# Three x tiles of the first attention batches transposed by DMA where TensorE and VectorE did it

## The chip, the cores and the metric

The kernel runs on one core of a Trainium2 chip. The metric is the device time of one execution in microseconds; before the change it is 313.5 us, the median of three runs (312.98 to 313.79). The profiled execution spans 311.5 us, and all positions in time below are counted from the start of that span.

## The reference

Causal attention with a decaying bias feeds a two-layer feed-forward network with exact GELU. The attention has 8 batches, 8 heads, 576 positions and 64 values per head; the network has 4608 tokens, a width of 512 and an inner width of 2048.

```python
scores = scale * q @ k.T + minimum(-(cum[i] - cum[j]), 0)   # cum = cumsum(max(s, 0))
attn   = softmax(where(j > i, -1e9, scores))
x      = (attn @ v).transpose(0, 2, 1, 3).reshape(4608, 512)
h      = x @ w_in
out    = (0.5 * h * (1 + erf(h / sqrt(2)))) @ w_out
```

Matmuls are done in bf16 with fp32 accumulation.

## The kernel before

The tokens are numbered batch after batch. Attention works on a batch b in query tiles `it` of 128 rows (tiles 0 to 3) and one of 64 rows (tile 4). The network works on nine chunks c of 512 tokens. Since a batch has 576 tokens, chunk 1 takes its columns 512 to 1023 from batch 0's tile 4 (columns 512 to 575), and from batch 1's tiles 0 to 3 (from column 576 on).

The program is one long stream, written out by hand under a manual schedule: each engine does its instructions in the order of the program, and semaphores join the engines. The loop `for c in range(NCH)` does layer 1 of chunk c, then layer 2 of chunk c with the attention of batch c + 1 placed between its matmuls. The lists `side[0]` to `side[15]` say what comes after each sixteenth of layer 2. For chunk 0, `groups(c, (0, 1), side[:8])` does layer 2's row blocks ("subs") 0 and 1 together with the first eight lists, and then sub 2 and sub 3 take four lists each.

The pieces that matter here:

- `sc_item` (sc): scores of four heads by TensorE (line 349), exponential by ScalarE (line 364). `mk_item` (mk): the causal mask, by VectorE (lines 372 and 377). `scale_v`: v times a weight, by VectorE (line 224).
- `av_item` (av): attention rows of one tile and four heads g, by TensorE (line 440); VectorE divides (lines 449 and 450) and writes x, of which there are six buffers. When the second group of heads (g = 1) of a tile is done, `to_xT` follows at once, unless the caller passes `later=True`.
- `to_xT` puts x, whose rows are tokens, into xT, whose rows are the 512 values of x: `xT[:, ko, token]`. With `pe=True` TensorE does four transposes into a PSUM tile (line 415) and VectorE copies it to xT (line 418). The PSUM tile shares two buffers with the attention rows (tag "av"). Without it SyncE issues one DMA transpose from x to xT (line 411).
- `l1_item`: layer 1, TensorE (line 472) and GELU by ScalarE (line 477). It reads all 512 columns of a chunk at once. `l2_item`: layer 2, TensorE (line 488). At the end of a sub ScalarE (chunk 0, line 498) or VectorE (line 500) copies to o_sb, of which there are three buffers, and SyncE stores it (line 502).
- GpSimd issues the loads of q, k and v and of the weights (lines 106, 122, 148). SyncE's queue holds the output stores and the DMA transposes, in the order of the program.

All tiles of batch 0, and tiles 0 to 3 of batch 1, are transposed by TensorE before the change. From tile 4 of batch 1 on, all go by DMA: 31 DMA transposes, of which the first is issued at 60.9 us.

Of the kernel before, what the change touches and what calls it, by code (L numbers as in the profile page):

```python
# [19 lines left out]
def kernel(  # L20
# [89 lines left out]
    def load_qks(b):  # L110
        load_qk(b, 0)
        load_qk(b, 1)
# [5 lines left out]
    def load_v(b, eng, sts=range(ST)):  # L118
        t = raws[b, "v"] if (b, "v") in raws else raw_v(b)
        for st in sts:  # L120
            n_st = 128 if st < ST - 1 else SL
            eng.dma_start(  # L122
                out=t[:n_st, st, :, :],
                in_=bass.AP(
                    tensor=v.tensor,
                    offset=v.offset + b * H * S * D + st * 128 * D,
                    ap=[[D, n_st], [S * D, H], [1, D]],
                ),
            )
# [56 lines left out]
    def tr_qk(b, i, g):  # L186

        nc.vector.transpose(  # L188
            qkT[b % 2][:, i, g, :S, :].rearrange("p s e -> p (s e)").bitcast(fp32)
            .rearrange("p (l j) -> p j l", j=LT),  # L190
            raws[b, "qk"][:, i, g, :].bitcast(fp32).rearrange("p (j w) -> p j w", j=LT),
        )
# [20 lines left out]
    def square_v(b, st):  # L213
        n_st = 128 if st < ST - 1 else SL
        sq = work.tile([128, H * D], bf16, tag="sq", bufs=2, name="sq")
        nc.scalar.activation(  # L216
            sq[:n_st], raws[b, "v"][:n_st, st].rearrange("p h d -> p (h d)"), func=AF.Square,
            accum_out=sumv[:n_st, b, st : st + 1],
        )

    def scale_v(b, st, eng=nc.vector):
        n_st = 128 if st < ST - 1 else SL
        w = wb[:n_st, st, b * H : (b + 1) * H]
        eng.tensor_tensor(  # L224
            vv[b % 2][:n_st, st, :, 0:D],
            raws[b, "v"][:n_st, st, :, :],
            w.unsqueeze(2).to_broadcast([n_st, H, D]),
            op=MULT,
        )

    def den_col(b):
        nc.vector.tensor_copy(vv[b % 2][:, :, :, D], wb[:, :, b * H : (b + 1) * H])
# [228 lines left out]
    def l1_item(c, f2, n0=0, n1=NB):  # L461
        if f2 == 0 and n0 == 0:
            gT_of[c] = work.tile([128, FT, NB], bf16, tag="gT", bufs=1, name="gT")
        if n1 - n0 < NB and f2 % 4 < 2:
            h_ps = yps.tile([128, 2, NB // 2], fp32, tag="mlp", bufs=2, name="h2_ps")
        else:
            h_ps = ps.tile([128, 2, NB], fp32, tag="sc", bufs=2, name="h_ps")
        h_ps = h_ps[:, :, : n1 - n0]
        for i in range(2):
            ft = f2 * 2 + i  # L470
            for ko in range(KO):
                nc.tensor.matmul(  # L472
                    h_ps[:, i, :], lhsT=w_in_r[:, ko, ft * 128 : (ft + 1) * 128],
                    rhs=xT[:, ko, c * NB + n0 : c * NB + n1],
                    start=(ko == 0), stop=(ko == KO - 1),
                )
        nc.scalar.activation(  # L477
            gT_of[c][:, f2 * 2 : f2 * 2 + 2, n0:n1], h_ps, func=AF.Gelu
        )
# [24 lines left out]
    def exp_set():  # L504
        nc.scalar.preload_act_table_set("natural_log_exp_and_others")  # L505
# [67 lines left out]
    sc, mk, av = sc_item, mk_item, av_item  # L573
# [5 lines left out]
    for c in range(NCH):  # L579
        b = c + 1  # L580
        if c > 0 and b + 1 < B:
            load_qks(b + 1)
            load_v(b + 1, nc.gpsimd)
        if c == 0:

            late = [
                [], [], [], [], [(av, 0, 0, 2), (av, 0, 1, 2)],
                [(av, 0, 0, 3), (av, 0, 1, 3)], [(to_xT, 0, 2, True), (to_xT, 0, 3, True)],
                [], [(scale_v, 0, 4), (av, 0, 0, 4)], [(av, 0, 1, 4)],
            ] + [[]] * 6  # L590
            for half in range(2):
                for f2 in range(FT // 2):
                    l1_item(0, f2, half * 256, half * 256 + 256)
                    for f, *a in late[8 * half + f2]:
                        f(*a)
                    if f2 % 2 and 3 <= 8 * half + f2 <= 11:
                        square_v(0, 4 * half + f2 // 2 - 1)
        else:
            for f2 in range(FT // 2):
                l1_item(c, f2)  # L600
                for g, it in late_of.get(c, [])[f2 : f2 + 1]:
                    av(c, g, it)
                if b < B and f2 < HG:
                    tr_qk(b, 0, f2)
                    tr_qk(b, 1, f2)
                if b < B and f2 == 2:
                    den_col(b)
                    for st in range(2):
                        scale_v(b, st)
                if b < B and f2 == 3:  # L610
                    for st in range(2, ST):
                        scale_v(b, st)
                if b < B and 4 <= f2 < 4 + HG:
                    absmax(b, f2 - 4)
                if c == 2 and f2 == 7:
                    cert_decay()
                if f2 < ST and c < B:
                    square_v(c, f2)
        if b < B:
            if c == 0:  # L620
                for g in range(HG):
                    for i in range(2):
                        tr_qk(b, i, g)
                den_col(b)
            exp_set()
            if c == 0:
                load_qks(2)
                load_v(2, nc.gpsimd)
                side = [[] for _ in range(16)]
                side[0] = [(sc, b, 0, 0), (mk, b, 0, 0)]  # L630
                side[3] = [
                    (sc, b, 1, 0), (to_xT, 0, 4, True), (scale_v, b, 0), (scale_v, b, 1), (mk, b, 1, 0)
                ]
                side[5] = [(sc, b, 0, 1), (av, b, 0, 0), (av, b, 0, 1)]
                side[6] = [(av, b, 1, 0, True), (av, b, 1, 1, True), (scale_v, b, 2), (mk, b, 0, 1)]
                side[7] = [(to_xT, b, 0, True), (sc, b, 1, 1)]
                side[8] = [(to_xT, b, 1, True), (scale_v, b, 3), (av, b, 0, 2), (gelu_set,), (mk, b, 1, 1)]
                side[9] = [(av, b, 0, 3)]
                side[11] = [(av, b, 1, 2, True), (scale_v, b, 4), (square_qk, 0, 0, 0), (square_qk, 0, 0, 1)]
                side[12] = [(av, b, 1, 3, True), (square_qk, 0, 1, 0), (square_qk, 0, 1, 1)]  # L640
                side[13] = [(to_xT, b, 2, True)]
                side[14] = [(to_xT, b, 3, True)]
                groups(c, (0, 1), side[:8])
                for sub in (2, 3):
                    groups(c, (sub,), side[4 * sub : 4 * sub + 4])
            else:

                side = [[] for _ in range(16)]
                sc_at = (1, 4, 6, 8) if b < 4 else (1, 4, 7, 10)
                for at, (g, u) in zip(sc_at, [(0, 0), (1, 0), (0, 1), (1, 1)]):  # L650
                    side[at].append((sc, b, g, u))
                side[sc_at[3]].append((gelu_set,))
                mk_at = (4, 6, 8, 10) if b < 4 else (4, 7, 10, 13)
                for at, (g, u) in zip(mk_at, [(0, 0), (1, 0), (0, 1), (1, 1)]):
                    side[at].append((mk, b, g, u))
                for at, (g, it) in zip((5, 6, 8, 9), [(0, 0), (0, 1), (1, 0), (1, 1)]):
                    side[at].append((av, b, g, it))
                if b < 4:
                    side[10].append((av, b, 0, 2))
                    side[11].append((av, b, 1, 2))  # L660

                    side[15].extend([(av, b, 0, 3), (av, b, 1, 3)])
                if c == 1:
                    side[0].append((absmax, c, 0))
                    side[12].extend([(square_qk, c, 1, 0), (square_qk, c, 1, 1)])
                    side[3].append((cert_exp,))
                for sub in range(4):
                    groups(c, (sub,), side[4 * sub : 4 * sub + 4])
        else:
            for sub in range(4):  # L670
                l2_item(c, (sub,), store=(c, sub) < LAST)
                if c == B - 1:
                    (cert_1, cert_2, cert_3, cert_4)[sub]()
                elif sub == 0:

                    rv = nc.values_load(bad[0:1, 0:1], min_val=0, max_val=1)
# [169 lines left out]
```

## Time and profile before

| what | value |
|---|---|
| time | 313.5 us (312.98 to 313.79) |
| span of the profiled execution | 311.5 us |
| TensorE transposes (line 415) | 36, for nine tiles |
| VectorE copies to xT (line 418) | 9: 424 ns for 128 rows, 292 ns for 64 |
| DMA transposes (line 411) | 31, median 2.4 us from issue to landing, longest 7.0 |
| layer 2 of chunk 0 | from 35.6 us |
| layer 1 of chunk 1 | from 55.34 us |

The page gives each engine's busy time as a share of the span. A matmul's record lasts from its start until its result is there, and the next starts before that, so TensorE's cost of a piece is read from its start to the start of the next piece. A row by time has the start, the length of the group, the engine, the line and the operation, and in brackets an idle time ahead of it with what ended it. In the DMA view q0 is the queue of the transfers that GpSimd issues and q1 that of SyncE's; "share" is the time their packets took, over 16 DMA engines, and since packets overlap it can be over 100%. Packets as small as four bytes are the semaphores' and not data.

### The profile page before, as it was taken

To read this page: it belongs to the slowest core of one execution; us is meant where nothing else is said; L and a number is where in the kernel's file an instruction comes from. 1 tells how busy PE (TensorE), PEld (TensorE's weight loads), DVE (VectorE), ACT (ScalarE), POOL (GpSimd) and SP (SyncE) were. 2 spreads that over 40 slices of the span, in tenths; PEclk is the share of its full clock that TensorE was granted. 3 is DMA by queue.
4 is the path that set the end of the run, shared out by engine and by line. 5 is a ranking of instruction groups with operands and counts; after the bars stand their busy time and mean duration, and the time that the engine had idled before them with its cause. 6 is when DMAs were issued, how large, how long until landed. Compare 5 with 4: busy or idle time off the path is not lost. (4 is left out here: it accounts for less than half of the span.)

```text
span 311.5 us, 6102 instructions
## 1 busy us (share of the span) xinstructions
PE 303.9 (98%) x2511; PEld 155.1 (50%) x2511; DVE 195.2 (63%) x397; ACT 193.3 (62%) x262; POOL 53.1 (17%) x72
## 2 busy tenths in 40 slices
PE   6999999999999999999999999999999999999994
PEld 2479755444554455445454545444544555444441
DVE  6786577697769775966498549955895632250010
ACT  1787878878848772974687548765776657105500
POOL 7473250142002400060007000500000000000000
PEclk9999999999999999999999999999999999999999
DMA  8999999769641974089208941623101311010012
GB/s 144 214 231 206 225 219 283 160 140 197 165 98 17 211 173 118 8 180 208 87 18 175 220 93 31 146 66 103 51 19 42 103 53 25 34 68 36 0 69 76
DMA packets 33027, 36.73 MB, mean 118 GB/s; under 512 B 17760, under 2 KB 22112, under 8 KB 32992
## 3 DMA queue, kind: packets, MB, share of 16 engines
q0 software_dynamic: 11472, 22.81, 37.5%
q1 hardware_dynamic: 20336, 12.93, 14.7%
q10 hardware_dynamic: 1184, 0.52, 0.6%
q8 instruction: 21, 0.34, 0.4%
q14 instruction: 14, 0.11, 0.1%
HBM read 36.85 MB, written 9.44 MB: 149 GB/s over the span
## 5 line engine op out<-in xcount | busy, mean ns | idle before, releaser
L488 PE MATMUL o_ps<-w_out_r,gT 128*128 128x512 bf16 x576 | 135.6, 379 | 0.0
L472 PE MATMUL h_ps<-xT,w_in_r 128*128 128x512 bf16 (+1 forms) x640 | 131.6, 358 | 0.0
L477 ACT ACTIVATE gT<-h_ps 128x1024 bf16<-128x1024 f32 (+1 forms) x80 | 75.1, 938 | 65.7 <-PE h_ps L472 64.7
L472 PEld LDWEIGHTS <-w_in_r 128*128 128x128 bf16 x640 | 60.0, 98 | 54.3 <-issue 0.3
L488 PEld LDWEIGHTS <-gT 128*128 128x128 bf16 x576 | 52.0, 98 | 56.9 <-issue 2.8
L364 ACT ACTIVATE P<-sc_ps 128x1024 bf16<-128x1024 f32 x56 | 54.3, 1021 | 25.3 <-PE sc_ps L349 25.2
L500 DVE COPY o_sb<-o_ps 128x512 f32<-128x512 f32 x30 | 20.7, 692 | 55.7 <-PE o_ps L488 55.7
L122 POOL DMA_DIRECT2D raw_v<-in_v_dram x39 | 33.1, 859 | 125.8 <-ACT sq L216 115.2
L188 DVE STREAM_TRANSPOSE qkT<-raw_qk 128x576 f32<-128x576 f32 x32 | 37.0, 1237 | 0.0
L449 DVE RECIPROCAL rc<-av 128x4 f32<-128x4 f32 (+1 forms) x80 | 14.1, 176 | 35.1 <-PE av L440 35.0
L450 DVE TENSOR_TENSOR x<-av,rc 128x256 bf16<-128x256 f32 (+1 forms) x80 | 33.8, 423 | 3.0
L440 PEld LDWEIGHTS <-P 128*128 128x128 bf16 x576 | 26.5, 98 | 15.8 <-DVE P L372 1.4
L208 DVE TENSOR_REDUCE amx<-raw_qk 128x2 f32<-128x2304 bf16 x13 | 32.6, 2534 | 0.0
L440 PE MATMUL av<-vv,P 128*128 128x65 bf16 x576 | 30.2, 193 | 0.1
L372 DVE TENSOR_TENSOR P<-P,tri_bf 128x1024 bf16<-128x1024 bf16 (+1 forms) x33 | 22.0, 670 | 6.6 <-ACT P L364 5.9
L224 DVE TENSOR_TENSOR vv<-raw_v,wb 128x512 bf16<-128x512 f32 (+1 forms) x39 | 25.2, 691 | 0.4 <-DMA raw_v<-in_v_dram 0.4
L216 ACT ACTIVATE sq<-raw_v 128x512 bf16<-128x512 f32 (+1 forms) x40 | 24.8, 621 | 0.0
L349 PE MATMUL sc_ps<-qkT 32*128 32x256 bf16 (+2 forms) x560 | 18.1, 250 | 0.0
L349 PEld LDWEIGHTS <-qkT 32*128 32x128 bf16 x560 | 11.8, 92 | 12.2 <-issue 8.9
L505 ACT ACT_TABLE_LOAD x8 | 10.3, 1283 | 1.3 <-PEq L830 1.2
L424 PE MATMUL f_ps<-zero 128*128 128x512 bf16 x30 | 9.7, 449 | 1.2 <-DVE zero L151 1.2
L508 ACT ACT_TABLE_LOAD x8 | 10.3, 1283 | 0.1
(80 smaller groups left out, 92.1 us busy)
## 6 DMA issues: line engine op xcount, KB each, us to landing
out_dram<-o_sb SPq DMA_DIRECT2D x34, 256.0 KB, 2.2
raw_v<-in_v_dram POOLq DMA_DIRECT2D x31, 256.0 KB, 5.6
raw_qk<-in_q_dram POOLq DMA_DIRECT2D x7, 576.0 KB, 7.5
raw_qk<-in_k_dram POOLq DMA_DIRECT2D x7, 576.0 KB, 10.7
w_in_r<-in_moe_w_in_dram POOLq DMA_DIRECT2D x4, 512.0 KB, 10.6
w_out_r<-in_moe_w_out_dram POOLq DMA_DIRECT2D x4, 512.0 KB, 16.8
raw_v<-in_v_dram POOLq DMA_DIRECT2D x8, 128.0 KB, 6.1
raw_qk<-in_q_dram POOLq DMA_DIRECT2D x2, 288.0 KB, 6.1
```

Of the source, the lines that this page charges most:

```text
L122: eng.dma_start(out=t[:n_st, st, :, :], in_=bass.AP(tensor=v.tensor, offset=v.offset + b * H * S * D + st * 128 * D, ap=[[D, n_st], [S * D ...
L188: nc.vector.transpose(qkT[b % 2][:, i, g, :S, :].rearrange("p s e -> p (s e)").bitcast(fp32) .rearrange("p (l j) -> p j l", j=LT), raws[b, ...
L208: nc.vector.tensor_reduce(amx[:, b * HG + g], raws[b, "qk"][:, :, g, :], axis=AX, op=ALU.max, apply_absolute_value=True,)
L216: nc.scalar.activation(sq[:n_st], raws[b, "v"][:n_st, st].rearrange("p h d -> p (h d)"), func=AF.Square, accum_out=sumv[:n_st, b, st : st ...
L224: eng.tensor_tensor(vv[b % 2][:n_st, st, :, 0:D], raws[b, "v"][:n_st, st, :, :], w.unsqueeze(2).to_broadcast([n_st, H, D]), op=MULT,)
L349: nc.tensor.matmul(s_ps[h // 2][:, h % 2, off : off + n], lhsT=qk[r, 1, g, jt * 128 : jt * 128 + 128, e], rhs=qk[r, 0, g, i0 : i0 + n, e], ...
L364: nc.scalar.activation(P[:, 2 * h2 : 2 * h2 + 2, o : o + 512], s_ps[h2], func=AF.Exp, scale=scale)
L440: nc.tensor.matmul(o_ps[:, h, :], lhsT=P[:, h, off : off + 128], rhs=vv[b % 2][:, jt, 4 * g + h, :], start=(i == 0), stop=(i == len(BLK[it ...
L450: nc.vector.tensor_tensor(x_of[b, it][:n, g * 256 : g * 256 + 256].rearrange("p (h d) -> p h d", d=D), o_ps[:n, :, 0:D], rc[:n].unsqueeze( ...
L472: nc.tensor.matmul(h_ps[:, i, :], lhsT=w_in_r[:, ko, ft * 128 : (ft + 1) * 128], rhs=xT[:, ko, c * NB + n0 : c * NB + n1], start=(ko == 0) ...
L477: nc.scalar.activation(gT_of[c][:, f2 * 2 : f2 * 2 + 2, n0:n1], h_ps, func=AF.Gelu)
L488: nc.tensor.matmul(y_of[c, sub], lhsT=gT[:, ft, sub * 128 : (sub + 1) * 128], rhs=w_out_r[:, ft, :], start=(ft == 0), stop=(ft == FT - 1),)
```

## The change

Three tiles that chunk 1 needs, tile 4 of batch 0 and tiles 0 and 1 of batch 1, are transposed by DMA in place of TensorE and VectorE. This is to take twelve transposes off TensorE and three copies off VectorE. The tiles of batch 1 are issued directly when their attention rows are done (`later` is no longer passed), tile 4 of batch 0 is moved from `side[3]` to `side[7]`. Tiles 2 and 3 of batch 1 stay as they were.

```diff
                 side[3] = [
-                    (sc, b, 1, 0), (to_xT, 0, 4, True), (scale_v, b, 0), (scale_v, b, 1), (mk, b, 1, 0)
+                    (sc, b, 1, 0), (scale_v, b, 0), (scale_v, b, 1), (mk, b, 1, 0),
                 ]
                 side[5] = [(sc, b, 0, 1), (av, b, 0, 0), (av, b, 0, 1)]
-                side[6] = [(av, b, 1, 0, True), (av, b, 1, 1, True), (scale_v, b, 2), (mk, b, 0, 1)]
-                side[7] = [(to_xT, b, 0, True), (sc, b, 1, 1)]
-                side[8] = [(to_xT, b, 1, True), (scale_v, b, 3), (av, b, 0, 2), (gelu_set,), (mk, b, 1, 1)]
+                side[6] = [(av, b, 1, 0), (av, b, 1, 1), (scale_v, b, 2), (mk, b, 0, 1)]
+                side[7] = [(to_xT, 0, 4), (sc, b, 1, 1)]
+                side[8] = [(scale_v, b, 3), (av, b, 0, 2), (gelu_set,), (mk, b, 1, 1)]
```

## The prediction

> **What bounds the kernel now.** I read the busy shares first, then the list of waits, then the stretch from 36 to 56 us, where layer 2 of chunk 0 runs: TensorE by time, SyncE by time, and the DMA queues by window.
>
> ```profile
> PE 303.9 (98%) x2511; PEld 155.1 (50%) x2511; DVE 195.2 (63%) x397; ACT 193.3 (62%) x262; POOL 53.1 (17%) x72
> ```
>
> TensorE is busy from end to end. Its queue is in order, so time taken out of it anywhere, or put in, moves the end by as much, unless a later idle place absorbs it. The list of waits has none of size on TensorE: its longest entries are other engines that wait for TensorE (ACT gT 64.7 us, DVE o_sb 55.7 us). Eight matmuls of chunk 1's layer 1 start at 57.31 us and the attention row behind them at 59.04: 1.73 us, 216 ns each, the full rate. So I find nothing later that gives time back.
>
> TensorE by time, in the stretch that is changed (start, length, engine, line, operation):
>
> ```profile
> 40.41 0.29 PE L415 MATMUL xt_ps<-ident_bf,x 64*128 64x64 bf16 x4
> 40.63 1.90 PE L488 MATMUL o_ps<-w_out_r,gT 128*128 128x512 bf16 x8
> ...
> 45.76 0.39 PE L415 MATMUL xt_ps<-ident_bf,x 128*128 128x128 bf16 x4
> 46.08 0.64 PE L349 MATMUL sc_ps<-qkT 32*128 32x256 bf16 x24
> ...
> 47.52 0.39 PE L415 MATMUL xt_ps<-ident_bf,x 128*128 128x128 bf16 x4
> 47.75 0.41 PE L440 MATMUL av<-vv,P 128*128 128x65 bf16 x8
> ...
> 54.48 1.03 PE L488 MATMUL o_ps<-w_out_r,gT 128*128 128x512 bf16 x4
> 55.34 1.03 PE L472 MATMUL h_ps<-xT,w_in_r 128*128 128x512 bf16 x4
> ```
>
> What counts is from start to next start, since the matmuls overlap: a tile's four transposes hold the queue for 0.22, 0.32 and 0.23 us. At 55.34 us chunk 1 begins; its first matmul reads xT columns 512 to 1023, to which all three changed tiles belong.
>
> The DMA engines in the same stretch, in two windows (queue: packets, MB, share):
>
> ```profile
> q0 software_dynamic: 293, 0.66, 110.8%
> ...
> out_dram<-o_sb SPq DMA_DIRECT2D x2, 256.0 KB, 8.2
> ```
>
> ```profile
> q0 software_dynamic: 350, 1.05, 67.6%
> q1 hardware_dynamic: 335, 0.62, 33.9%
> ...
> out_dram<-o_sb SPq DMA_DIRECT2D x1, 256.0 KB, 6.6
> ```
>
> The first is 46 to 49 us, the second 49.5 to 55 us. q0 carries GpSimd's loads (q, k and v of batch 2, issued from 36.6 to 46.4 us, landing 12 to 13.5 us later); q1 carries what SyncE issues. Two output stores were issued at 46.37 us, yet until 49 us q1 has no packet at all: nearly 3 us in which the loads ahead are served. From then on q1 gets about one packet for each of q0. So these stores land 7.3 and 8.2 us after issue (53.7 and 55.0 us), where the whole kernel's median is 2.2. The DMA share is above 1.0 until 54 us, 0.63 in 55 to 56 and 0.40 in 56 to 57.
>
> **What the Trainium skill says.** "VectorE: DVE Perf Modes", section The three transpose paths, prices one 128x128 bf16 transpose at 390 ns on TensorE and 1309 ns by DMA. The trace has the same order of size: 0.39 us for four overlapping on TensorE, 1.19 us of SyncE's queue for one DMA transpose of a whole tile. "DMA: Bandwidth & Descriptors", section Queues, rings and completion order, says that a DMA engine alternates between the queues that have work, packet by packet; the 335 against 350 packets above agree. "TensorE: Matmul & The Clock Gate", Part 1, says that TensorE's clock halves after an idle window of some 3.4 us and comes back after about as long busy. The opening agrees in part: the warming matmuls (line 424) run at 4 per us from 2 to 5 us, then 7 in the next, and after the idle from 6.30 to 8.45 us the rate is still full.
>
> **The change part by part.**
>
> *Removed from TensorE:* twelve transposes of three tiles, 0.22 + 0.32 + 0.23 = 0.77 us of queue. The attention matmuls that follow at 48.85 us take 0.38 us for eight, where the like ones take 0.24; they wait for scale_v of tile 3 (ending at 48.97 us), which sits behind the two removed copies on VectorE (0.42 us each). With these gone that 0.14 us goes too. Sum 0.9 us. The attention matmuls at 44.30 us still wait 0.24 us for x, as before.
>
> *Removed from VectorE:* copies of 0.29 + 0.42 + 0.42 = 1.13 us. VectorE idles here for other engines (3.9 us before the mask at 39.70), so beyond the 0.14 they are worth nothing.
>
> *Moved:* three tiles go to SyncE's queue. The order of instructions of the changed kernel there is: transpose (1,0), transpose (1,1), store of sub 0, store of sub 1, transpose (0,4), store of sub 2. Its waits show the first weight load of chunk 1 waiting for exactly the three transposes. Behind that weight load, on TensorE's in-order queue, stands all of layer 1 of chunk 1, hence GELU on ScalarE, and the late attention rows that VectorE reads.
>
> *When TensorE asks:* 55.34 - 0.9 = 54.4 us.
>
> *When the tiles are there:* x of (1,0) is written at 45.27 us, of (1,1) at 45.82, both some 0.2 earlier now. Issues: 45.1 and 46.3 us (1.2 us each, from the two at 81.60 us that take 2.50), stores from 47.5, transpose (0,4) at about 48.4. It is the oldest tile but the last in the queue, behind both stores. The nearest row is the one DMA transpose under load, of 64 rows too, with nothing ahead of it on SyncE's queue:
>
> ```profile
> xT<-x SPq DMA_TRANSPOSE x1, 7.0
> ```
>
> It was issued at 60.89 us. Unloaded ones land after 2.4. That would put (1,0) at 52.1 us or later, and (0,4), were it alone, at 48.4 + 7.0 = 55.4.
>
> Lower bound for (0,4): before, the second store landed at 55.0 us. Its queue now starts 1.3 us earlier (45.1 for 46.37) but has two whole transposes ahead, which at the unloaded pace of 1.25 us each are 2.5: 56.2. Then the half transpose, about 0.6 at that pace: 56.8 us. Upper bound: the 256-byte packets of the transposes (about 512 for a whole tile, by the 1104 packets under 512 B around the pair at 81.6, so 32 on each of 16 engines) alternate one for one with the loads' packets, of which about 28 per engine are left at 48 us (98 in the us before 49, 350 in 49.5 to 55, over 16), so the first transpose is done only when the loads are, at 55.5; then the second (1.0), two stores (1.0 each), the half one (0.6) and the way to the semaphore, 0.8: 60 us. If several small packets pass for each large one it is nearer the lower. I take 58.2, a little under the middle, 58.4.
>
> *Net:* chunk 1 starts at 58.2 and not 55.34: +2.9 us; TensorE idles 58.2 - 54.4 = 3.8 us. For the clock I take nothing, as the windows of the skill's page are fixed in time and an idle of 3.8 us rarely holds a whole one; the other end is the opening's loss, 3.5 us at half rate, 1.75 us.
>
> **The rivals.**
>
> *A, forecast: the wait is longer than what is saved.* 313.5 + 2.9 = 316.4 us. For it: the packets and landings above. Against it: one lone transpose under load is the only one seen.
>
> *B, the same with a fallen clock and the late bound.* 60 - 55.34 = 4.7, plus 1.75: 320.0 us. GpSimd's next loads, issued at 56.63 us before, would lengthen it. Against it: TensorE idles over 5 us only at the upper bound.
>
> *C, the transposes hide.* If small packets pass freely, they land by 54.4 us and the whole 0.9 is kept: 312.6 us. For it: loads end by 56 us anyway, and a transpose moves only 128 KB. Against it: the store now behind two transposes landed at 55.0 without them.
>
> *D, they land at about 55.3 us* and the wait replaces what was saved: 313.5 us. Nothing in the trace favours so exact a tie.
>
> **How the numbers follow.** A 0.77, B 0.09, C 0.09, D 0.05. A spans 314.6 to 318.6. The range reaches down into D's neighbourhood, 313.4, and up towards B, 319.4; C lies outside and about half of B, together some 0.14. Slower by over 0.3% (0.94 us) means a landing after 56.3 us: A and B, 0.86, less a little of A's lower edge: 0.85. C's 0.9 us is just under 0.3%, so it counts mostly as the same: 0.11 same, 0.04 faster.
>
> **What would show it.** Right: in the list of waits TensorE's weight load at line 472 idle for 2.4 to 5.5 us before chunk 1, released by DMA; SyncE's three transposes landing after 7 us and more, the 64-row one last; no transposes at line 415 at 40, 45 and 47 us; after the wait the same spacing as before. If matmuls there come at 4 per us, the clock fell. Wrong: landings of 3 to 5 us, or the wait given back in a place where TensorE waits now and I saw none. The weakest step is the landing time of (0,4), since it is inferred from two stores and one half transpose.

## The result and the profile after

The changed kernel takes 325.0 us (median of six runs, 322.6 to 328.5), the kernel before 313.3 us beside it: a ratio of 1.0359, 95% interval 1.0298 to 1.042. The ratio leaves out the slowest of the six runs, which lies over 1.5% above the fastest, and stands for 11.2 us; the medians are 11.7 us apart. The kernel is slower, as forecast, but by almost four times the 2.9 us of the forecast.

The page of the changed kernel: busy shares, and the slices of TensorE's clock.

```profile
PE 304.1 (94%) x2458; PEld 155.4 (48%) x2499; DVE 194.5 (60%) x394; ACT 193.4 (60%) x262; POOL 53.0 (16%) x72
...
PEclk9799999669999999999999999999999999999998
```

TensorE's busy time is all but unchanged (304.1 us for 303.9), but the span is longer, and the clock was below full in three slices: one in the opening (about 8 to 16 us), two at 57 to 73 us. Two rows of the changed kernel's list of waits follow (engine, line, what it waited for: total us, times, longest). The first names the reason; the second is ScalarE waiting for a buffer whose store was late too:

```profile
PE h_ps L472 <- DMA xT<-x: 9.4, 1, 9.4
...
ACT o_sb L498 <- DMA out_dram<-o_sb: 5.0, 1, 5.0
```

TensorE by time at the start of chunk 1, and SyncE by time:

```profile
55.53 1.03 PE L488 MATMUL o_ps<-w_out_r,gT 128*128 128x512 bf16 x4
65.99 1.01 PE L472 MATMUL h_ps<-xT,w_in_r 128*128 128x512 bf16 x2 [9.43 <-DMA xT<-x]
67.22 2.34 PE L472 MATMUL h_ps<-xT,w_in_r 128*128 128x512 bf16 x5 [0.22 <-issue]
...
72.00 8.37 PE L472 MATMUL h_ps<-xT,w_in_r 128*128 128x512 bf16 x37
```

```profile
46.94 2.62 SPq L411 DMA_TRANSPOSE xT<-x  x2
49.60 1.11 SPq L502 DMA_DIRECT2D out_dram<-o_sb  x2
50.75 4.91 SPq L411 DMA_TRANSPOSE xT<-x  x1
```

The three transposes land 13.2 to 15.1 us after issue, the 64-row one last: 50.75 + 15.1 = 65.9, where TensorE starts. (A few matmuls are missing from each trace: the x2 and x5 above stand for eight.) That last transpose also holds SyncE for 4.91 us in place of 1.2. By window (its length; busy time and count of TensorE, its weight loads, VectorE, ScalarE and GpSimd; TensorE's granted clock; DMA share; GB/s):

```profile
54.00:56.00 2.00, 2.00 (x17) 1.17 (x16) 0.93 (x3) 2.00 (x3) 0.00 (x0) 1.00 0.75 70
...
60.00:62.00 2.00, 0.00 (x0) 0.00 (x0) 0.00 (x0) 0.00 (x0) 0.00 (x0) 0.51 1.11 261
...
66.00:68.00 2.00, 1.78 (x4) 0.70 (x6) 0.00 (x0) 0.00 (x0) 0.00 (x0) 0.50 1.10 238
...
70.00:72.00 2.00, 2.00 (x17) 0.95 (x15) 1.93 (x4) 1.27 (x4) 0.00 (x0) 0.93 0.33 61
```

The clock falls to a half during the wait and stays there for some four us of work. From the two profiles the difference of 324.8 - 311.5 = 13.3 us splits so. (1) The opening: the same warm-up matmuls ran at half rate in this execution, so the first scores start at 12.35 us and not 10.70: +1.65. (2) From there to the end of chunk 0's layer 2, 44.04 us and not 44.64: -0.60, the saving. (3) Waiting, from 56.39 to 65.99: +9.60. (4) From the first matmul of chunk 1 to the third group of layer 1 (72.00), 6.01 us where it was 3.94 (55.34 to 59.28): +2.07, the clock. The sum is 12.7; 0.6 is left unassigned. Item (1) belongs to no edit:

```profile
8.86 2.32 PE L424 MATMUL f_ps<-zero 128*128 128x512 bf16 x5
...
12.35 0.63 PE L394 MATMUL sc_ps<-qkT 32*128 32x256 bf16 x8
```

```profile
8.87 1.25 PE L424 MATMUL f_ps<-zero 128*128 128x512 bf16 x5
...
10.70 0.63 PE L394 MATMUL sc_ps<-qkT 32*128 32x256 bf16 x8
...
59.28 4.91 PE L472 MATMUL h_ps<-xT,w_in_r 128*128 128x512 bf16 x22
```

The first is the changed kernel, the second the kernel before: five equal matmuls at two rates. In the profiles of all twelve experiments below, variants of the changed kernel among them, these five run at the full rate. Whether the changed kernel's other five runs began slowly can't be read from them; (2) + (3) + (4) = 11.1 is close to the 11.2 us of the ratio.

### The profile page after: what moved, and what is told of

The parts are those of the page before. It is cut to its first block, busy times and chain, and to the rows that moved or that the text cites. A ratio compares the mean times of both kernels' runs of the same rounds, so it can differ in the third digit from the quotient of the medians.

```text
span 324.8 us, 6043 instructions
## 1 busy us (share of the span) xinstructions
PE 304.1 (94%) x2458; PEld 155.4 (48%) x2499; DVE 194.5 (60%) x394; ACT 193.4 (60%) x262; POOL 53.0 (16%) x72
## 5 line engine op out<-in xcount | busy, mean ns | idle before, releaser
L488 PE MATMUL o_ps<-w_out_r,gT 128*128 128x512 bf16 x552 | 132.0, 379 | 2.3 <-issue 1.6
L349 PEld LDWEIGHTS <-qkT 32*128 32x128 bf16 x560 | 11.8, 92 | 12.7 <-issue 9.9
L498 ACT ACTIVATE o_sb<-o_ps 128x512 f32<-128x512 f32 x5 | 2.9, 597 | 15.6 <-PE o_ps L488 10.6
L424 PE MATMUL f_ps<-zero 128*128 128x512 bf16 x29 | 10.8, 509 | 1.2 <-DVE zero L151 1.2
```

Source lines behind the costliest of these rows:

```text
L349: nc.tensor.matmul(s_ps[h // 2][:, h % 2, off : off + n], lhsT=qk[r, 1, g, jt * 128 : jt * 128 + 128, e], rhs=qk[r, 0, g, i0 : i0 + n, e], ...
L488: nc.tensor.matmul(y_of[c, sub], lhsT=gT[:, ft, sub * 128 : (sub + 1) * 128], rhs=w_out_r[:, ft, :], start=(ft == 0), stop=(ft == FT - 1),)
```

## The experiments

**Is it the transposing, or any transfer in that place?** The three transposes become plain copies of the same bytes.

```diff
-nc.sync.dma_start_transpose(out=xT[:, :, t0 : t0 + n], in_=x[:n, :])
+nc.sync.dma_start(out=xT[:, :, t0 : t0 + n], in_=x.rearrange("t (p c) -> t p c", c=128))
+# (64-row tile: two copies, one for each half of the partitions)
```

> The three DMA transposes are replaced by plain copies between the same tiles, in runs of 256 bytes (128 bytes for the 64-row tile), so that nothing is transposed and xT holds other values; queue, bytes, waits and order stay. Theory X (under the loads it is the transposing itself that is slow, and it slows the loads too): the copies land some 7 to 9 us after issue, TensorE waits less than 3 us, and the time is 313.5 to 317 us. Theory Q (any transfer of many small packets behind the loads would do the same): they land after 13 to 15 us and the time stays at 322 to 328 us.

Measured: 320.2 us, ratio 1.0220 (1.0195 to 1.0245). It lies between the two answers. TensorE waits 5.74 us:

```profile
59.92 1.01 PE L483 MATMUL h_ps<-xT,w_in_r 128*128 128x512 bf16 x2 [5.74 <-DMA xT<-x]
```

The two whole copies land 12.2 and 12.6 us after issue, nearly as late as transposes: so queueing behind the loads makes most of the wait, and theory X in its pure form falls. But Q in its pure form falls too, since by the ratios some 4.4 us of the change's loss is gone. To compare the DMA queues, the transposes have to be issued at the same time as the copies, since the loads run on by themselves. In the changed kernel's own profile they were issued 2.1 us later, when less of the loads was left (from 52 to 60 us 0.70 MB of them passed, at 116 GB/s in all). A run further below, with 36 idle matmuls that come after the issues, has them at 44.81 us, and the copies are at 44.80. Its DMA view from 50 to 58 us first, then that of the copies:

```profile
DMA packets 1373, 1.40 MB, mean 175 GB/s; under 512 B 1062, under 2 KB 1062, under 8 KB 1373
...
q0 software_dynamic: 381, 1.13, 67.6%
q1 hardware_dynamic: 992, 0.26, 48.5%
```

```profile
DMA packets 1903, 1.98 MB, mean 248 GB/s; under 512 B 1326, under 2 KB 1326, under 8 KB 1903
...
q0 software_dynamic: 396, 1.17, 66.7%
q1 hardware_dynamic: 1507, 0.81, 41.7%
```

The loads move nearly as much beside transposes as beside copies (1.13 MB for 1.17), so X's second half, that they slow the loads, is not seen here. It is SyncE's own queue that falls behind: 992 packets for 1507. From the share, over 16 engines and 8 us, one of its packets took 63 ns on average with transposes and 35 with copies. How much that delays a landing differs from run to run: in this run the last transpose was there by 60.7 us, only 0.8 after the 59.92 of the copies, while the changed kernel with 24 idle matmuls, issued at much the same time, has its last at 64.2. Why a transpose's packets take longer here was not found out. The 64-row tile isn't quite like for like, as its copies have runs of 128 bytes.

**Without the loads.** Batch 2's loads are left out.

```diff
-load_qks(2)
-load_v(2, nc.gpsimd)
+# buffers touched by a 2-element memset; batch 2 reads batch 1's q, k and v
+raws[2, "qk"], raws[2, "v"] = raws[1, "qk"], raws[1, "v"]
```

> The changed kernel without batch 2's loads of q, k and v: batch 2 is computed from batch 1's data, so those three loads are left out. To be read against the run of the kernel before with the same omission. If the loads in flight are the cause (X and Q both): the transposes land within 5 us, TensorE does not wait, the time is 0.5 to 0.9 us under that of the kernel before with the omission. Theory S (the transposes are slow because of their own queue, behind stores and one another): the wait stays over 5 us and this run is 5 us or more above that one.

> The kernel before without batch 2's loads of q, k and v (batch 2 computed from batch 1's data). All theories: TensorE never waits for these loads, so within 0.5 us of the kernel before, 313 to 313.8 us. It is the control for the run of the changed kernel with the same omission.

Measured: 323.3 us (1.0303, 1.0275 to 1.0331) and 313.5 us (1.0005, 0.999 to 1.0021). That seemed to speak for S, but the omission took no load out of the stretch. GpSimd by time in the first of them:

```profile
34.13 0.12 POOL L629 MEMSET raw_v<- 128x2 f32 x1
36.20 0.71 POOL L106 DMA_DIRECT2D raw_qk<-in_q_dram  x1 [1.96 <-DMA w_out_r<-in_moe_w_out_dram]
38.61 0.71 POOL L106 DMA_DIRECT2D raw_qk<-in_k_dram  x1 [1.70 <-DMA w_out_r<-in_moe_w_out_dram]
40.00 1.77 POOL L122 DMA_DIRECT2D raw_v<-in_v_dram  x2 [0.68 <-DMA raw_v<-in_v_dram]
```

Batch 3's loads found the buffers free and took batch 2's place. So the pair doesn't test the loads; it shows only that the loss doesn't depend on whose they are. Batch 3's loads were then held back as well:

```diff
+if c == 1:
+    nc.gpsimd.tensor_copy(gate, ssq[:, 1, 1:2])   # waits for ScalarE's square, about 56 us
 if c > 0 and b + 1 < B:
     load_qks(b + 1)
```

> The changed kernel without batch 2's loads (batch 2 computed from batch 1's data), and with batch 3's loads held back until ScalarE has squared batch 0's k, some 56 us, by one small GpSimd copy that reads the square's sum; so that no load is in flight on GpSimd's queue from about 47 to 56 us. If loads in flight are the cause (X and Q): the transposes land within 5 us, TensorE does not wait for them, and the time is 0.5 to 0.9 us under the control (313.5 us): 312.6 to 313.0. Theory S (their own queue): the wait stays, 318 us or more.

Measured: 312.6 us, ratio 0.9986 (0.9974 to 0.9999), where the kernel before has 313.2. The DMA view from 44 to 52 us, and TensorE by time:

```profile
q1 hardware_dynamic: 1529, 0.83, 39.6%
q0 software_dynamic: 27, 0.06, 3.6%
...
xT<-x SPq DMA_TRANSPOSE x3, 3.4
```

```profile
53.97 1.03 PE L489 MATMUL o_ps<-w_out_r,gT 128*128 128x512 bf16 x4
54.83 1.89 PE L473 MATMUL h_ps<-xT,w_in_r 128*128 128x512 bf16 x7
```

With q0 all but empty the same transposes, the last behind the same stores, land in 2.3 to 4.3 us, and chunk 1 follows layer 2 with no gap. S is refuted: without the loads in flight there is no wait. The 0.56 us between the medians is near the saving, but it isn't shown to be that: the kernel before was not run with the same hold, and in this profile TensorE waits 0.60 us for w_out at 43.74 us.

**What the clock costs.** Idle matmuls on TensorE while it waits.

```diff
+if c == 1:
+    filler(24)     # second run: filler(36)
 for f2 in range(FT // 2):
     l1_item(c, f2)
```

> The changed kernel with 24 idle matmuls (5.2 us at full rate) ahead of layer 1 of chunk 1, where TensorE waits, so that its clock stays up. If the fall of the clock costs what the half rate from 66 to 70.3 us shows: 2.1 us less than the changed kernel, about 323 us where it has 325. If the clock's fall costs nothing beyond the wait: no change. If the wait is shorter than 5.2 us in a run, that run gets longer instead.

> The changed kernel with 36 idle matmuls (7.8 us at full rate) ahead of layer 1 of chunk 1; 24 had ended 4.6 us before the transposes landed, and the clock fell all the same. If the fall costs about 2.2 us: the clock stays at 1.0 where the wait after the fill is short, and the time is 320.5 to 323 us, the changed kernel's 325.0 less 2 to 2.5. If not: 325.

Measured: 322.5 us (1.0278, 1.0213 to 1.0344) with 24, 323.0 us (1.0312, 1.0266 to 1.0358) with 36. With 24, in the profiled run, the fill ended 4.6 us before the transposes landed, and the clock fell all the same. With 36 it covers the wait in the profiled run, and ends 1.3 us after the last landing:

```profile
54.27 7.93 PE L424 MATMUL f_ps<-zero 128*128 128x512 bf16 x36
62.04 1.89 PE L472 MATMUL h_ps<-xT,w_in_r 128*128 128x512 bf16 x8
63.77 0.41 PE L440 MATMUL av<-vv,P 128*128 128x65 bf16 x8
```

Eight matmuls take 1.73 us after it, the full rate. By the ratios the fill gains 2.5 us with 24 and 1.5 with 36, about the 2.07 of the trace, but the intervals overlap with the changed kernel's, since the landing itself varies: the times don't prove it. Of the eight runs with a fill, the four with a mean clock of 0.996 and above took 320.0 to 321.5 us, the four with 0.991 to 0.993 took 324.2 to 324.9. That doesn't part the two either, as a late landing lengthens the wait and brings the clock down. The price of the clock rests on the trace.

**Which of the three, and how many.** Only the 64-row tile by DMA; only the two whole tiles; only the 64-row tile, but early.

```diff
 # only half: side[6], side[8] as in the kernel before, and
+side[7] = [(to_xT, 0, 4), (to_xT, b, 0, True), (sc, b, 1, 1)]
 # only two: (to_xT, 0, 4, True) back in side[3], and
+side[7] = [(sc, b, 1, 1)]
 # half early: the kernel before, without (to_xT, 0, 4, True) in side[3], and
+side[0] = [(to_xT, 0, 4), (sc, b, 0, 0), (mk, b, 0, 0)]
```

> Only the 64-row tile (batch 0, tile 4) goes by DMA, behind the two stores; tiles 0 and 1 of batch 1 are transposed by TensorE as in the kernel before. Q: behind 16 packets of stores per DMA engine and 16 of its own it lands some 10 us after issue, near 57 to 58 us: TensorE waits 2 to 3 us, 315 to 316.5 us. X: if what costs is the transposing under load, about a fifth of the packets of the change is left, and the loads are hardly slowed: the same or less. If the long wait comes with the number of transposes and not with the place in the queue, then no wait: 313.3 us.

> Only tiles 0 and 1 of batch 1 go by DMA, ahead of the stores; the 64-row tile is transposed by TensorE as before. Q (the plain copies had the first two landing 12.4 us after issue): they land near 58 us, TensorE waits 3 to 4 us, with the clock's fall 317 to 320 us. X on top: near 60 to 62 us, 319 to 323 us. If the 64-row tile behind the stores sets the wait of the changed kernel alone: at most 315 us.

> Only the 64-row tile by DMA, at the head of layer 2 of chunk 0, with the loads as they were; tiles 0 and 1 of batch 1 by TensorE. Behind the two stores it landed after 11.7 us and cost 5.8 us. Q: with no store ahead but more loads it lands 10 to 15 us after issue, by 50 us at the latest, so no wait, and its four transposes are saved: 313.0, 0.2 us under the kernel before, which is no difference that the measurement can show. X: the loads beside it are slowed, but TensorE waits for none of them: the same. If it lands after 54.5 us all the same: 316 us or more.

Measured: 319.0 us (1.0170, 1.0126 to 1.0214), 319.6 us (1.0200, 1.0183 to 1.0217) and 313.6 us (1.0008, 0.999 to 1.0026). A single half tile in the wrong place already costs 5.3 us by the ratio. It lands 11.7 us after issue; TensorE waits 3.47 us, and the clock falls after that (window, its length, TensorE's busy time and count, clock, DMA share, GB/s):

```profile
58.00:59.00 1.00, 0.01 (x1) 1.00 1.06 213
...
60.00:61.00 1.00, 1.00 (x5) 0.67 1.04 187
61.00:62.00 1.00, 1.00 (x11) 0.50 1.07 196
```

The two whole tiles, with no store ahead of them, land after 12.6 and 13.8 us and bring a wait of 4.51 us; no one tile is to blame. The half tile issued at 30.8 us, by contrast, lands after 6.5, long before it is needed, and the time is that of the kernel before. It too went beside loads, so loads alone don't make a landing of 12 us and more. In its profile, one of its slower runs (314.9 us), TensorE waits elsewhere instead (list of waits):

```profile
PE o_ps L488 <- DMA w_out_r<-in_moe_w_out_dram: 1.0, 1, 1.0
...
PE av L440 <- DVE vv L224: 0.4, 1, 0.4
```

Those are loads that came late. The run with the loads held back waits 0.60 us for w_out too, with no transpose ahead of it, so how much of this the early transpose caused is open.

**A version that hides them.** Batch 2's v loaded later, and then the half tile early as well.

```diff
-load_v(2, nc.gpsimd)
 side[11] = [(av, b, 1, 2, True),
+    (late_v,),      # a GpSimd copy of one column of x(1, 2), then load_v(2)
```

> The changed kernel with batch 2's v loaded later: a small GpSimd copy that reads x of tile 2 of batch 1 (written at about 52 us) stands ahead of its five loads. Nothing is left out. Only the rest of w_out and q and k of batch 2 (landing until 49 to 53 us) then stand beside the transposes. X and Q: the transposes land by 52 to 56 us, so the wait is 0 to 2 us and the time 312.5 to 315.5 us. S: no change, 322 to 328 us.

> The late load of batch 2's v, and besides the 64-row tile's DMA transpose put at the head of layer 2 of chunk 0 (issued near 33 to 36 us) in place of behind the two stores; nothing is left out. With v late alone the first two landed at 53.6 and 54 us and the 64-row one at 56.0, which set a wait of 1.25 us. If the place in the queue and the loads are the whole cause: it lands by 50 us, the two others by 54, no wait, 0.4 to 0.7 us under the kernel before: 312.5 to 312.9. If a transpose under load slows what is beside it so that others come later: a wait of 1 us or more is left and the time is 313.2 or above.

> The kernel before with batch 2's v loaded late, as in the variants of the changed kernel. The control for them. If the late load costs nothing by itself: 313.0 to 313.5 us, the same as before. If v comes too late for VectorE in chunk 1: above 314 us, and this much is no matter of the transposes.

Measured: 314.6 us (1.0041, 1.0024 to 1.0059), 313.2 us (0.9995, 0.9982 to 1.0007) and 313.3 us (0.9987, 0.9972 to 1.0002). Issuing five of the loads later removes all but 1.25 us of the wait; with the half tile early it is gone:

```profile
53.56 1.03 PE L489 MATMUL o_ps<-w_out_r,gT 128*128 128x512 bf16 x4
54.42 1.89 PE L473 MATMUL h_ps<-xT,w_in_r 128*128 128x512 bf16 x8
```

It equals the kernel before and doesn't beat it; 312.5 to 312.9 us had been expected. In its profile the stretch from the first scores to chunk 1 does take 0.57 us less (10.35 to 54.42, where it was 10.70 to 55.34), but the times don't show it, nor do they tell it from its control, the kernel before with late loads: a saving of half a microsecond is about what these intervals resolve.

## Why the prediction was right or wrong

**Right:** TensorE is the bound; chunk 1's first weight load waits for the three tiles; the 64-row tile, behind both stores, lands last; nothing later gives the time back. Rivals C and D (hidden, or a tie) are refuted. B, the fallen clock with a late landing, was nearest, and got a chance of 0.09.

**Wrong, the landing of (0,4).** This is the step that failed. Forecast: issued at 48.4 us and there 9.8 us later, at 58.2, between a lower bound of 56.8 and an upper of 60. In the changed kernel's profile it is issued at 50.75 and there 15.1 us later, at 65.9; less the opening's 1.65 that is 49.1 and 64.3. The upper bound took the loads' packets as passing at the pace that they have alone, and a transpose's packets as costing on top what they cost unloaded (1.0 us a tile). With plain copies this came out near: they were there at 59.92, or at 60.7 on the time scale of the kernel before, as that run's first scores began 0.77 us earlier. With transposes it was too low: on the same scale the last tile is there at 61.2, 64.3, 64.6 and 65.7 in the four profiles with all three tiles and the loads. SyncE's queue passed 992 packets beside the loads where with copies it passed 1507. The forecast had one transpose under load to go by, of half a tile, and said that this step was the weakest; it drew a range from it that was too narrow all the same. The wait was 9.6 us for 3.8. Why transposes pass so slowly there stays open.

**Wrong, the clock.** Taken as nothing, with 1.75 us as the other end. The Trainium skill, "TensorE: Matmul & The Clock Gate", Part 1, gives an idle window of some 3.4 us; I argued that 3.8 us of waiting rarely hold a whole one. In the half tile's profile the clock fell after a wait of 3.47 us. With 9.6 us it fell too, and cost 2.07.

**Too large, the saving.** 0.9 us forecast; 0.60 in the trace. The third group of scores starts sooner, and then has to wait, by the look of it for a score buffer. In the changed kernel, ScalarE and TensorE's weight loads by time:

```profile
42.14 1.94 ACT L364 ACTIVATE P<-sc_ps 128x1024 bf16<-128x1024 f32 x2 [0.84 <-PE sc_ps L349]
```

```profile
43.87 0.10 PEld L349 LDWEIGHTS <-qkT 32*128 32x128 bf16 x3 [0.42 <-issue]
44.13 0.51 PEld L349 LDWEIGHTS <-qkT 32*128 32x128 bf16 x21 [0.17 <-issue]
```

The exponentials end at 44.08, and only then do the other weight loads follow: the group takes 0.82 us where it took 0.60, which is what the 64-row tile's four transposes had cost (0.22). A further 0.09 us goes ahead of the fourth group. The 0.14 us at scale_v did come:

```profile
50.04 0.41 PE L440 MATMUL av<-vv,P 128*128 128x65 bf16 x8
50.50 1.67 PE L488 MATMUL o_ps<-w_out_r,gT 128*128 128x512 bf16 x7
```

Seven of eight matmuls are recorded; with the missing one, 0.22 us earlier, that place takes 0.24 us where it took 0.38. So 0.91 - 0.22 - 0.09 = 0.60.

## What to carry to other kernels

A transfer that moves work off the bound engine is worth what it saves only if it lands before the consumer's turn in the worst traffic of that stage, so read the landing time of its neighbours in the same microseconds, not the median of the kernel. A saving of 0.6 us was paid with a wait of 9.6, because loads that nobody needed yet kept the DMA engines busy. If it must be done, issue the transfer long before it is needed, or hold the load back behind it, though here neither beat the kernel before; and count an idle TensorE twice, for the wait and for the clock.

## What the runs showed of the hardware

- DMA transposes beside GpSimd's loads landed late: 11.9 to 15.9 us after issue in the four profiles with all three tiles and the loads, 2.3 to 4.3 with the loads held back. At equal times of issue the DMA engines moved 175 GB/s with transposes where plain copies of the same bytes left 248; the loads nearly kept their pace (1.13 MB for 1.17), SyncE's queue didn't (992 packets for 1507). Loads beside it are not enough, though: the half tile issued at 30.8 us landed after 6.5, and its queue's packets took 29 ns (288 in 16 us, a share of 3.3%).
- Under load three us and more pass before a newly issued transfer's first packet. From 46 to 51 us in the changed kernel q1 has only 7 packets, all of them after 50, though its first transpose was issued at 46.94.
- The Trainium skill, "DMA: Bandwidth & Descriptors", section Queues, rings and completion order, has a DMA engine take turns between its queues packet by packet. For each packet of the loads q1 passed 1.0 before the change (335 for 350), 2.6 with transposes (992 for 381) and 3.8 with copies. So a turn isn't one packet of this trace, or a queue at times had nothing ready; the runs don't tell which.
- The clock can fall after work has begun again: with the half tile alone the matmuls resume at 58.99 us and the clock is 1.00 up to 60 us, then 0.50 from 61.
- The opening's warm-up can end in either rate. After an idle of 1.76 us the changed kernel's matmuls ran at half rate; in the other thirteen profiles, after idles of 0.25 to 2.15 us, they ran at full: 1.65 us that no edit made.
